# A gated pair of S4D convolutions on one core: phases rounded inside the matmul chain, decay grids on GpSimd, trig in place in PSUM

## The chip, the core and the metric

The kernel runs on one core of one Trainium2 chip. A core has a matrix engine (PE, with its weight loads, PEld), a vector engine (DVE), a scalar engine for functions (ACT), GpSimd (POOL) and a queue engine that only starts transfers (SP). Each runs its own instructions in order and waits for the others on semaphores. Matmuls write PSUM, of which there are eight banks of 512 float32 per partition; everything else lives in SBUF. The metric is the device time in microseconds of the whole program, from its first instruction to its last.

## The reference, cut to what matters

Two diagonal state space layers A and B see the same input x (2048 steps, 512 channels, 128 modes a channel) and are mixed by a gate for each step.

```python
def layer(u, log_A_real, A_imag, C_real, C_imag, log_dt, D_skip):
    dt = exp(log_dt)
    A = -exp(log_A_real) + 1j * A_imag
    C = (C_real + 1j * C_imag) * dt[:, None]
    P = exp((A * dt[:, None])[:, :, None] * arange(L))    # 512 x 128 x 2048
    K = 2 * einsum("dn,dnl->dl", C, P).real               # the filter
    y = irfft(rfft(u, 2 * L) * rfft(K, 2 * L))[:L]
    return y + u * D_skip
g = sigmoid((x * gate_w).sum(-1, keepdims=True))
return g * layer_A(x) + (1 - g) * layer_B(x)
```

## The kernel before, in words

A channel of one layer is a filter; there are 1024. They are worked off in 64 units of 16 filters (`u`), 16 blocks of four units (`b`), 8 chunks of eight units (`c`) and 4 super-blocks of four blocks (`sb`).

Each filter is split as step = 64 m + q. Modes lie on the partitions, so that the sum over modes is a matmul of two factors, f1 (32 values of m) and f0 (64 of q), each a decay times a cosine or sine.

- Per chunk, `prep_ops(c)` (line 153) turns the parameters into an amplitude, a decay rate and phase factors. The phase factors are split into three bfloat16 parts (`split`, `rest`), written to DRAM (`bounce`) and read back turned (`back`) into `rot`. Most of it is DVE work on 128x128 tiles, with some ACT. `make_bases` (284) makes 28 columns of exponentials on ACT in seven parts; `amplitudes` multiplies four of them on DVE.
- Per unit, `phase` (298) makes 1024 phases, in turns, with two matmuls of 512 columns (unit 0 takes another way, with nine). `turn` (315) converts them to int16 on ACT, `half` (319) casts that to fp16 on DVE, and `less` (322) subtracts the whole turns with two more matmuls. `sine`, `absf` and `cosine` (334 to 342) are ACT passes over 1024 elements into the SBUF tile `fsn`. `grid1` and `grid0` (345 to 359) multiply exponentials into decay grids of 512 and 1024 elements on DVE; `prod1`, `prod_minus`, `prod_cos` and `prod_sin` (362 to 385) multiply grids and trig on DVE, two SBUF operands each.
- `modes` (387) sums over the modes with 32-column matmul tiles; `keep` and `skip` evacuate; `s1_k` and `keep_x` do the first step of a transform.
- Per block, `s2` (443) does the second step, `products` (466) multiplies the spectrum of the filter by that of the input in `v`, once straight and once crossed, in one DVE instruction for each of eight groups; four accumulating DMAs from POOL's queue (`add_products`, 498) add the two halves; `inverse` and `keep_z` transform back. Every second block a new `v` is made: `keep_v`, two kinds of DMA and, on ACT, `negate_v`.
- Per super-block, `final` and `final_out` finish and write; the last super-block has its own end (`last_e` to `last_out`). The gate is a matmul (591), a sigmoid over 2048 elements and sixteen DMAs that spread it over the partitions.

PSUM before: two banks for the phases, one each for `pk`, `ps1` and `fin`, three shared by the rest. The order of PE, DVE and ACT is that of one list, sorted by a key for each operation (the table `AT`, offsets against the unit's or block's number); a dependency without a semaphore ties each instruction to the one before it on its engine. Transfers and POOL's few instructions keep the order in which that list reaches them.

Of the kernel before, what the change touches and what calls it, by code (L numbers as in the profile page):

```python
# [11 lines left out]
BF16 = mybir.dt.bfloat16  # L12
I32 = mybir.dt.int32
F16 = mybir.dt.float16
I16 = mybir.dt.int16
# [4 lines left out]

M = 32
# [7 lines left out]
BUFS = {"f1": 2, "f0": 2, "fsn": 2, "ph": 1, "pk": 1, "ps1": 1, "bg": 3, "fin": 1}  # L37

# [7 lines left out]
def tile_gated_s4d(ctx: ExitStack, tc: tile.TileContext, nsb, a, out):  # L46
    nc = tc.nc
    nblk = 4 * nsb
    nunit = 4 * nblk
    nchunk = 2 * nsb  # L50

    const = ctx.enter_context(tc.tile_pool(name="const", bufs=1))
    prep = ctx.enter_context(tc.tile_pool(name="prep", bufs=1))
    work = ctx.enter_context(tc.tile_pool(name="work", bufs=2))
    psum = ctx.enter_context(tc.tile_pool(name="psum", bufs=1, space=PSUM))
    dram = ctx.enter_context(tc.tile_pool(name="dram", bufs=2, space=DRAM))

    V, S, PE = nc.vector, nc.scalar, nc.tensor
    ops = []

    def op(name, home, fn, i=None, *args):
        at = AT[name] if i is None else AT[name][i]
        ops.append((home + at, len(ops), name, fn, args, (name, i), home))

    def op_at(name, key, fn, *args):
        ops.append((key, len(ops), name, fn, args, None, key))


    small = const.tile([128, nchunk + 1 + nsb], F32, name="small")
    nc.sync.dma_start(out=small, in_=a["small"])  # L70
    ldt, sgn, gw = small[:, 0:nchunk], small[:, nchunk : nchunk + 1], small[:, nchunk + 1 :]
    pars, uraws = {}, {}

    def load_pars(c):
        pars[c] = prep.tile([128, 4, 128], F32, name="par", tag="par")
        nc.sync.dma_start(out=pars[c], in_=a["par"][c])

    def load_u(b):
        uraws[b] = work.tile([128, 8, Q], F32, name="uraw", tag="uraw", bufs=1)
        nc.sync.dma_start(out=uraws[b], in_=a["us"][b])  # L80

    load_pars(0)
    warm = const.tile([128, 1], F32, name="warm")
    V.memset(warm, 0.0)
    S.activation(warm, warm, AF.Exp)
    ident = const.tile([128, 128], F32, name="ident")
    ph0 = work.tile([16, 3, 512], BF16, name="ph0", tag="f1", bufs=BUFS["f1"])
    nid = const.tile([128, 128], F16, name="nid")
    w1 = const.tile([128, 2, 128], F32, name="w1")
    cph = const.tile([96, 2, 512], BF16, name="cph")  # L90
# [3 lines left out]
    consts = [(ident, a["ident"]), (ph0, a["ph0"]), (nid, a["nid"]), (w1, a["w1"]), (cph, a["cph"])]  # L94
    consts += [(dl, a["dl"]), (mi, a["mi"])]
    consts += [(gk[:, j : j + 8], a["gk"][:, j : j + 8]) for j in range(0, M, 8)]
    for i, (o, x) in enumerate(consts):
        op("ld", 0, lambda o=o, x=x: nc.sync.dma_start(out=o, in_=x), i)


    v = const.tile([128, M, 128], F32, name="v")
# [6 lines left out]
    gs = const.tile([128, 2048], F32, name="gs")  # L108
    eg = const.tile([128, Q, 2, M], F32, name="eg")


# [40 lines left out]

    def prep_ops(c):

        d = {}

        def tiles():
            if d:
# [664 lines left out]
```

## Time and profile before

| | us |
|---|---|
| median of 3 runs | 607.37 (606.05 to 607.65) |
| the profiled execution: its span | 606.9 |
| of it: DVE busy | 505.4 |
| ACT busy | 502.6 |
| PE busy | 491.7 |
| POOL busy | 61.0 |

The profile is of one execution. Its span runs from the first to the last instruction; no longer time of that execution is given, so the span is its own time. Busy time is the time in which at least one instruction of the engine runs. Ends of matmuls are modelled, and a busy PE includes the filling of its array. In a view of groups, a row names the line, engine, operation, the tile written and those read, the shape and the count, then the busy time of the group in microseconds and the mean of one instruction in nanoseconds, then the idle time of the engine before them with what ended it. In a view of the timeline, a row starts with the start and the length in microseconds of one or more instructions of a line that ran without a gap.

### The profile page before, as it was taken

Reading aid. Unit: us, or ns where it says so; the run is one execution under the profiler, and the core shown is the slowest. Engines: PE = TensorE matmul, PEld = TensorE weight load, DVE = VectorE, ACT = ScalarE, POOL = GpSimd, SP = SyncE. Lnnn points to the kernel's source line nnn. Section 1 sums busy time; section 2 is a strip of 40 time slices with the busy share of each in tenths; the row PEclk is TensorE's granted clock in tenths of the full one; section 3 lists DMA queues with packets and bytes.
Section 4 is the critical chain, followed back from the end, with each engine's and each line's share of the span. In section 5 each row is a group of like instructions: output and inputs, shape, how many; then the busy total and the mean of one; then the engine's idle time right before and its main releaser. Section 6 shows DMA issues by size and latency. Waiting matters only on the chain.

```text
span 606.9 us, 22768 instructions
## 1 busy us (share of the span) xinstructions
PE 491.7 (81%) x10071; PEld 393.6 (65%) x10071; DVE 505.4 (83%) x872; ACT 502.6 (83%) x942; POOL 61.0 (10%) x72
## 2 busy tenths in 40 slices
PE   5587869695987969987695979998688888988756
PEld 4454747584775857776474857777466775767656
DVE  6599999977998978998799778998699786898930
ACT  3999998888998978799788989799698897786611
POOL 0000100202002100012002020020102020020720
PEclk9799999988898979999899888999699898999989
DMA  8956440635008260185306251073502651054441
GB/s 281 292 171 84 97 98 3 106 53 115 20 2 125 51 134 21 27 138 88 78 3 106 53 123 38 30 115 64 114 1 43 101 98 44 21 89 80 72 69 72
DMA packets 91923, 50.39 MB, mean 83 GB/s; under 512 B 75840, under 2 KB 80448, under 8 KB 91824
## 3 DMA queue, kind: packets, MB, share of 16 engines
q1 hardware_dynamic: 86704, 32.15, 23.1%
q0 software_dynamic: 5120, 16.78, 16.5%
q8 instruction: 79, 1.29, 0.9%
q14 instruction: 20, 0.16, 0.1%
HBM read 16.93 MB, written 5.77 MB: 37 GB/s over the span
## 4 chain that ended last, share of the span: by engine, by line
PE 18%; ACT 14%; DMA 13%; DVE 9%; issue 3%; POOL 1%; ACTq 0%; POOLq 0%; DVEq 0%
DMA xall<-xall 6%; DMA dsp<-sp 4%; PE psi L513 4%; PE ps L455 4%; DVE xall L468 3%; DMA rot<-dsp 3%; ACT bas L289 2%; PE pf L540 2%; ACT r L317 2%; PE pk L393 2%; DVE f L375 2%; PE ps L411 2%; ACT fsn L338 2%; PE ph L325 1%; ACT fsn L342 1%
## 5 line engine op out<-in xcount | busy, mean ns | idle before, releaser
L347 DVE TENSOR_TENSOR f<-bas 128x1024 f32<-128x1024 f32 (+1 forms) x128 | 119.0, 947 | 3.1 <-ACT bas L289 3.1
L455 PE MATMUL ps<-xall,gk 128*64 128x64 f32 (+1 forms) x1728 | 113.9, 252 | 5.5 <-ACT v L479 2.3
L455 PEld LDWEIGHTS ps<-xall,gk 128*64 128x64 f32 (+1 forms) x1728 | 102.9, 153 | 19.5 <-ACT v L479 4.0
L513 PE MATMUL psi<-mi,xall 128*128 128x128 f32 x512 | 80.9, 310 | 31.1 <-DMA xall<-xall 31.1
L502 POOL DMA_DIRECT2D xall<-xall x64 | 53.4, 1248 | 522.9 <-ACT r L317 188.9
L513 PEld LDWEIGHTS psi<-mi,xall 128*128 128x128 f32 x512 | 75.0, 221 | 41.4 <-issue 35.5
L468 DVE TENSOR_TENSOR xall<-ps,v 128x512 f32<-128x512 f32 x128 | 85.6, 683 | 6.1 <-PE ps L455 3.4
L317 ACT ACTIVATE r<-ph 128x1024 int16<-128x1024 f32 x64 | 67.0, 1047 | 25.3 <-PE ph L312 23.7
L411 PE MATMUL ps<-w,ks 128*64 128x128 f32 x1024 | 70.5, 280 | 15.3 <-DVE ks L405 8.1
L375 DVE TENSOR_TENSOR f<-f,fsn 128x1024 f32<-128x1024 f32 x64 | 78.0, 1220 | 1.4 <-ACT fsn L342 1.4
L363 DVE TENSOR_TENSOR f<-f,fsn 128x1024 f32<-128x1024 f32 x64 | 77.9, 1218 | 0.0
L393 PE MATMUL pk<-f,f 128*32 128x64 f32 x4096 | 75.3, 229 | 2.1 <-DVE f L385 1.0
L393 PEld LDWEIGHTS pk<-f,f 128*32 128x32 f32 x4096 | 64.4, 115 | 17.8 <-issue 6.1
L338 ACT ACTIVATE fsn<-ph 128x1024 f32<-128x1024 f32 x64 | 67.2, 1050 | 5.7 <-PE ph L325 5.6
L411 PEld LDWEIGHTS ps<-w,ks 128*64 128x64 f32 x1024 | 55.3, 138 | 25.0 <-DVE ks L405 10.2
L342 ACT ACTIVATE fsn<-fsn 128x1024 f32<-128x1024 f32 x64 | 69.8, 1091 | 0.3
L335 ACT ACTIVATE fsn<-ph 128x1024 f32<-128x1024 f32 x64 | 67.5, 1055 | 0.1
L289 ACT ACTIVATE bas<-dec 128x128 f32<-128x128 f32 x224 | 60.6, 482 | 0.1
L519 ACT COPY z<-psi 128x512 f32<-128x512 f32 x64 | 38.4, 617 | 25.5 <-PE psi L513 25.5
L320 DVE CAST r<-r 128x1024 f16<-128x1024 int16 x64 | 27.1, 423 | 37.0 <-ACT r L317 36.9
L312 PE MATMUL ph<-cph,rot 96*128 96x512 bf16 x126 | 39.2, 393 | 21.5 <-DMA rot<-dsp 15.5
L325 PE MATMUL ph<-r,nid 128*128 128x512 f16 x128 | 41.8, 410 | 15.9 <-DVE r L320 15.4
(102 smaller groups left out, 595.7 us busy)
## 6 DMA issues: line engine op xcount, KB each, us to landing
xall<-xall POOLq DMA_DIRECT2D x64, 256.0 KB, 6.5
v<-v SPq DMA_DIRECT2D x64, 128.0 KB, 4.5
uraw<-in_us SPq DMA_DIRECT2D x16, 256.0 KB, 3.5
z<-in_ut SPq DMA_DIRECT2D x16, 256.0 KB, 5.7
out_dram<-ot SPq DMA_DIRECT2D x24, 128.0 KB, 2.6
par<-in_par SPq DMA_DIRECT2D x8, 256.0 KB, 2.6
gk<-in_gk SPq DMA_DIRECT2D x4, 512.0 KB, 5.3
eg<-in_eg SPq DMA_DIRECT2D x4, 512.0 KB, 7.2
```

Of the source, the lines that this page charges most:

```text
L289: S.activation(bases[c][:, :, j], decays[c][:, 0], AF.Exp, scale=-float(s) if s else 0.0)
L317: S.activation(rs[u].bitcast(I16), phs[u], AF.Copy)
L338: S.activation(fsn(u)[:, 0], phs[u], AF.Abs)
L342: S.activation(f, f, AF.Sin, bias=HALF_PI, scale=-TWO_PI)
L347: V.tensor_tensor(o.rearrange("p k (a b) -> p k a b", b=8), bas[:, :, hi : hi + n].unsqueeze(3).to_broadcast([128, 16, n, 8]), bas[:, :, l ...
L363: V.tensor_tensor(f1s[u].rearrange("p v k m -> p v (k m)"), f1s[u][:, 1].rearrange("p k m -> p (k m)").unsqueeze(1).to_broadcast([128, 2, ...
L375: V.tensor_tensor(f0[:, :, :, 0:32], f0[:, 1, :, 0:32].unsqueeze(1).to_broadcast([128, 2, 16, 32]), back, OP.mult)
L393: PE.matmul(pk[32 * kd : 32 * kd + 32, i, :], f1[:, p, 4 * i + kd, :], f0[:, p, 4 * i + kd, :], start=p == 1, stop=p == 0, tile_position=( ...
L411: PE.matmul(ps[64 * ri : 64 * ri + 64, i, :], kss[u][:, i, :], w1[:, ri, :], start=True, stop=True, tile_position=(0, 64 * ri),)
L455: PE.matmul(ps[h : h + w, j, 0:n], gk[:, k, h : h + w], xall[:, x0:x1, 2 * k : 2 * k + 2], start=True, stop=True, tile_position=(0, h),)
L468: V.tensor_tensor(k.rearrange("p x (k t) -> p k x t", t=2), p2s[b, g][:, :, 0:64].unsqueeze(2).to_broadcast([128, 4, 2, 64]), v[:, 4 * g : ...
L513: PE.matmul(ps[:, i, :], xk(b)[:, x : x + 2, :].rearrange("p x k -> p (x k)"), mi, start=True, stop=True)
```

## The change

It rewrites most of the kernel around the same mathematics. What it does, part by part:

- Phases. They are rounded inside the accumulation: the matmul chain of each 512-element half adds 1.5 x 2^23, adds the phase, subtracts 1.5 x 2^23 and subtracts the phase again. `turn`, `half` and `less` go. Phase factors are two fp16 parts. The half that belongs to f0 uses rows 0 to 63 of the array, that of f1 rows 64 to 127; four matmuls each, alternating.
- Trig. Each half has one bank for its phases, in which the sine replaces them, and one for the absolute value, which the cosine replaces. The two banks change roles from unit to unit (`t0`, `t1` and `u0`, `u1`). The products read them there.
- Grids. `grid0` and `grid1` run on POOL, two SBUF operands each, and so do `amplitudes`; of the 28 exponentials the four with shift 0 are constants.
- Prep. Chunks 1 and 2, 3 and 4, 5 and 6 are prepared together; except for the first batch the arithmetic that touches no PSUM runs on POOL.
- `products` becomes two instructions for each group, straight and crossed; `v` is laid out in four planes; `negate_v` moves to DVE.
- The gate's matmul writes all 128 rows, the sigmoid works in PSUM, and its sixteen spreading DMAs go.
- PSUM: four banks for trig, one for `pk`, and three that all else takes in a listed turn (`SLOTS`). One list of 2494 numbers (`ORDER`) gives the order of all operations, and the ties without semaphore now also bind POOL's instructions and SP's transfers.

```diff
+ONE_W, ONE_M, LOW = 4096.0, 3072.0, 2048.0
+BATCHES = ((0,), (1, 2), (3, 4), (5, 6), (7,))
+ORDER = [
+    11, 6, 1, 3, 0, 2, 5, 4, 74, 45, 40, 50, 43, 41, 44, 46, 42, 18, 19, 20, 21, 22, 24, 12, 23,
...
+    def prep_ops(i):
+        cs = BATCHES[i]
+        w = len(cs)
+        E = V if i == 0 else G
...
+        def high():
+            S.activation(halves(0), both("tb"), AF.Copy)
+
+        def rest():
+            E.tensor_tensor(both("tb"), both("tb"), halves(0), OP.subtract)
...
+    def turns(c):
+        i = next(i for i, cs in enumerate(BATCHES) if c in cs)
+        for h, t in zip((0, 64), dsps[i]):
+            src = t[BATCHES[i].index(c)].rearrange("(u k) d n -> (k d) u n", u=8)
+            dma(rot[h : h + 32 * (1 + h // 64), c % 2], src)
+
+    def make_bases(c):
+        for j, s in enumerate(SHIFTS):
+            if s:
+                S.activation(bas[:, c % 2, :, j], decays[c][:, 0], AF.Exp, scale=-float(s))
...
     def phase(u):
-        for h in range(2):
-            PE.matmul(ph[:, 512 * h : 512 * h + 512], rot[:, u % 8, :], cph[:, h, :], start=True, stop=True)
+        p0s[u], p1s[u] = (bank(f"{k}{u % 2}", f"{k}{u % 2}") for k in "tu")
+        for j in range(4):
+            for h, ps in ((0, p0s[u]), (64, p1s[u])):
+                w = rot[:, u // 8 % 2, u % 8] if j % 2 else ones
+                PE.matmul(
+                    ps, w[h : h + 64], cph[h : h + 64, j], start=j == 0, stop=j == 3, tile_position=(h, 0)
+                )
+
+    def magnitude(u, ps, pc, k):
+        pc[u] = bank(f"{k}{1 - u % 2}", f"{k}{1 - u % 2}")
+        S.activation(pc[u], ps[u], AF.Abs)
+
+    def sine(u, ps):
+        S.activation(ps[u], ps[u], AF.Sin, scale=TWO_PI)
+
+    def cosine(u, pc):
+        S.activation(pc[u], pc[u], AF.Sin, bias=HALF_PI, scale=-TWO_PI)
...
     def grid(u, o, hi, n, lo):
-        V.tensor_tensor(
+        G.tensor_tensor(
...
+    def sin_plus(u):
         o = f0s[u][:, 1, :, 32:64]
-        V.scalar_tensor_tensor(o, o, -1.0, g0(u)[:, 1], op0=OP.mult, op1=OP.mult)
+        V.scalar_tensor_tensor(o, o, -1.0, half(u, p0s[u], False), op0=OP.mult, op1=OP.mult)
+
+    def one_cos(u):
+        f = f1s[u].rearrange("p v k m -> p v (k m)")
+        V.tensor_tensor(f[:, 0], f[:, 1], p1c[u], OP.mult)
...
+    def products(b, g, second):
+        x0 = 64 * (b % 2)
+        if second:
+            x0 = 32
+        k = xall[:, x0 : x0 + 32, 8 * g : 8 * g + 8]
+        vv = v[:, 2 * (b % 2) + second, 4 * g : 4 * g + 4, :]
...
+    def negate_v(i, h):
+        V.tensor_scalar(v_at(hi, i, 1, h), v_at(hi, i, 0, h), -1.0, None, op0=OP.mult)
...
+    def gate_sig(j):
+        S.activation(psg[j], psg[j], AF.Sigmoid, scale=sgn)
...
+    for n in ORDER or range(len(ops)):
+        key, name, fn, args = ops[n]
...
         for i in new:
-            if i.engine in (mybir.EngineType.PE, mybir.EngineType.DVE, mybir.EngineType.Activation):
-                if i.engine in last:
...
+            if i.engine in last:
...
+    cph = np.zeros((2, 64, 4, 512))
...
+    cph[:, 0, 0], cph[:, 0, 2] = ONE_M, -ONE_M
+    cph[:, :, 3] = -cph[:, :, 1]
```

More of the change, by code (lines that the diff above doesn't have):

```diff
@@ L93, in tile_gated_s4d @@
     mi = const.tile([128, 128], F32, name="mi")
[L94 to L101, printed above, removed]
+    v = const.tile([128, 4, M, 32], F32, name="v")
     xall = const.tile([128, 128, 2 * M], F32, name="xall")
@@ L144, in make_dt @@
         ]
[L147 to L174 removed]
+    als, decays, dsps = {}, {}, {}
@@ new lines, in prep_ops @@
+        return start + middle + [
+            add("t2", "t2", "rc"), high, rest, low, bounce,
+            mul("mx", "mx", "ax"), mul("ay", "ay", "sy"), diag, turned, dec,
+        ]
+    def turns(c):
[7 more added lines that the diff above has]
+                S.activation(bas[:, c % 2, :, j], decays[c][:, 0], AF.Exp, scale=-float(s))
```

719 lines of the change are left out of this document (345 added, 374 removed), and 153 rows, old and new, of the table ORDER.

## The prediction

> **What bounds it now.** I read the page's engine shares first, then the windows cut where the first and the last unit's mode products start (line 393, from its source view), then the groups kept apart by shape.
>
> ```profile
> span 606.9 us, 22768 instructions
> PE 491.7 (81%) x10071; PEld 393.6 (65%) x10071; DVE 505.4 (83%) x872; ACT 502.6 (83%) x942; POOL 61.0 (10%) x72
> L393 PE MATMUL pk<-f,f x4096: 218/219/316, 36.6 to 573.0; 128*32 128x64 f32 x196
> 0.00:36.60 36.60, 21.29 (x185) 14.49 (x188) 23.05 (x83) 26.13 (x61) 0.20 (x4) 0.91 0.88 280
> 36.60:572.10 535.50, 448.55 (x9387) 358.24 (x9386) 472.27 (x774) 466.78 (x864) 55.06 (x63) 0.95 0.38 71
> 572.10:607.00 34.90, 21.89 (x506) 20.88 (x504) 10.10 (x18) 9.71 (x19) 5.73 (x6) 0.90 0.26 62
> 151.70:221.90 70.20, 58.54 (x1127) 46.85 (x1126) 63.40 (x106) 65.27 (x118) 6.66 (x8) 0.94 0.37 66
> ```
>
> The columns of a window are its length, then the busy microseconds of PE, weight loads, DVE, ACT and POOL with instruction counts, granted clock, DMA share and GB/s. The reader is to see three stretches. The first 36.6 us load and prepare; the last 34.9 us are a chain of one block that has nothing beside it (PE 21.9, DVE 10.1, ACT 9.7). Between them lie 535.5 us for the 63 further units, 8.50 us each, where DVE (472.3) and ACT (466.8) are both 87 to 88% busy, PE 84% and POOL 10%. In the fullest chunk shown ACT reaches 65.27 of 70.20 us, 93%. So no engine waits for one culprit; two engines are nearly full, and the rest is what in-order queues lose to each other. The waits that one can name are small:
>
> ```profile
> PE psi L513 <- DMA xall<-xall: 31.1, 15, 7.4
> PE ph L312 <- DMA rot<-dsp: 15.5, 6, 3.9
> ```
>
> The first is mostly the last block's (7.4 of it) and the accumulating DMA's landing, which stays. The second is the phase factors returning from DRAM at the start of a chunk, six times; the new order prepares two chunks in one batch, so it should mostly go.
>
> **The change, engine by engine.** DVE first.
>
> ```profile
> L468 DVE TENSOR_TENSOR xall<-ps,v 128x512 f32<-128x512 f32 x128 | 85.6, 683 | 6.1 <-PE ps L455 3.4 <-DMA v<-v 2.4
> L375 DVE TENSOR_TENSOR f<-f,fsn 128x1024 f32<-128x1024 f32 x64 | 78.0, 1220 | 1.4 <-ACT fsn L342 1.4
> L363 DVE TENSOR_TENSOR f<-f,fsn 128x1024 f32<-128x1024 f32 x64 | 77.9, 1218 | 0.0
> L347 DVE TENSOR_TENSOR f<-bas 128x1024 f32<-128x1024 f32 x64 | 77.4, 1211 | 0.0
> L381 DVE TENSOR_TENSOR f<-f,fsn 128x512 f32<-128x512 f32 x64 | 43.9, 685 | 11.3 <-ACT fsn L342 11.1
> L385 DVE SCALAR_TENSOR_TENSOR f<-f,fsn 128x512 f32<-128x512 f32 x64 | 43.7, 682 | 0.0
> L347 DVE TENSOR_TENSOR f<-bas 128x512 f32<-128x512 f32 x64 | 43.6, 683 | 3.1 <-ACT bas L289 3.1
> L320 DVE CAST r<-r 128x1024 f16<-128x1024 int16 x64 | 27.1, 423 | 37.0 <-ACT r L317 36.9
> L244 DVE RECIPROCAL rc<-rc 128x128 f32<-128x128 f32 x8 | 7.5, 943 | 0.0
> L213 DVE TENSOR_TENSOR tb<-tb,sp 128x256 f32<-128x256 f32 x16 | 6.7, 420 | 0.0
> ```
>
> The two grids leave: 77.4 + 43.6 = 121.0. The cast of line 320 leaves: 27.1. The four trig products (77.9 + 78.0 + 43.9 + 43.7 = 243.5) become six of 512 elements, one operand in PSUM; line 468 has that form, 85.6/128 = 0.669 each, so 384 x 0.669 = 256.9: +13. Line 468's 128 products become 256 of 256 elements. No such form with PSUM is shown; bounds are half of line 468 (0.33, no change) and line 213's 0.42 for 256 elements, which I take: 107.5, +22. The prep on DVE, by windows over the whole run for lines 183, 187 and 190:
>
> ```profile
> 0.00:607.00 607.00, 24.08 (x88) 0.94 0.41 83
> 0.00:607.00 607.00, 8.83 (x40) 0.94 0.41 83
> 0.00:607.00 607.00, 9.02 (x32) 0.94 0.41 83
> ```
>
> That is 24.1 + 9.0 + 8.8, with lines 244 and 213 another 7.5 + 6.7: 56. Seven of eight chunks leave for POOL, 49, but per later batch three operations (0.42 each), a reciprocal of twice 943 ns, a sign pass (0.42) and a PSUM copy (0.67) stay: 4 x 4.3 = 17, so -32. The 32 negations of v come over from ACT, some 0.4 each: +14. DVE: -121 - 27 + 13 + 22 - 32 + 14 = -131, in the middle 472 becomes 341.
>
> ACT:
>
> ```profile
> L342 ACT ACTIVATE fsn<-fsn 128x1024 f32<-128x1024 f32 x64 | 69.8, 1091 | 0.3
> L335 ACT ACTIVATE fsn<-ph 128x1024 f32<-128x1024 f32 x64 | 67.5, 1055 | 0.1
> L338 ACT ACTIVATE fsn<-ph 128x1024 f32<-128x1024 f32 x64 | 67.2, 1050 | 5.7 <-PE ph L325 5.6
> L317 ACT ACTIVATE r<-ph 128x1024 int16<-128x1024 f32 x64 | 67.0, 1047 | 25.3 <-PE ph L312 23.7 <-PE ph L306 1.2
> L289 ACT ACTIVATE bas<-dec 128x128 f32<-128x128 f32 x224 | 60.6, 482 | 0.1
> L418 ACT COPY xall<-ps 128x512 f32<-128x512 f32 x64 | 38.8, 606 | 1.3 <-PE ps L411 1.3
> L490 ACT ACTIVATE v<-v 64x512 f32<-64x512 f32 x32 | 18.3, 619 | 0.3
> ```
>
> Line 317's conversion leaves; sine, absolute value and cosine of 1024 become six passes of 512 from PSUM to PSUM. Before: 69.8 + 67.5 + 67.2 + 67.0 = 271.5. After: 384 at line 418's 0.606 (a 512 read from PSUM) = 232.7, so -39. The bounds are half of line 335 (0.527, 202: -69) and 0.67 where each cosine waits for its own absolute value with nothing between (257: -14). Of 28 exponentials a chunk four fall away: 60.6 x 32/224 = -8.7. Negations: -18.3. ACT: -66, the middle 467 becomes 401.
>
> PE:
>
> ```profile
> 162.58 0.59 PE L312 MATMUL ph<-cph,rot 96*128 96x512 bf16 x2 [0.21 <-ACT fsn L335]
> 163.99 1.10 PE L393 MATMUL pk<-f,f 128*32 128x64 f32 x64
> 165.08 0.59 PE L325 MATMUL ph<-r,nid 128*128 128x512 f16 x2
> 553.16 1.40 PE L455 MATMUL ps<-xall,gk 128*64 128x64 f32 x32
> ```
>
> A unit now has two pairs of 512 columns (phase and its correction), 0.59 + 0.59 = 1.18 us. It gets eight of 512 columns, alternating between the upper and lower 64 rows. In a pair the second adds 0.59 less one matmul's 0.38 to 0.39 = 0.21. If the halves run side by side there are four steps, 0.59 + 2 x 0.21 = 1.01: -11 us over 64 units. If not, 0.59 + 6 x 0.21 = 1.85: +43. No row shows row groups; the nearest shows column groups: 64 products of 64 columns in four column groups take 1.10 (17 ns each), 32 in two groups 1.40 (44 ns each), so groups of the array do overlap. I take -11: PE 449 becomes 438.
>
> POOL:
>
> ```profile
> L502 POOL DMA_DIRECT2D xall<-xall x64 | 53.4, 1248 | 522.9 <-ACT r L317 188.9 <-ACT ot L549 127.8 <-ACT v L479 78.4
> L561 POOL MEMSET el<- 128x2048 f32 x4 | 8.0, 2135 | 1.8 <-DVE f L375 1.2 <-PE pk L393 0.6
> ```
>
> POOL has done no arithmetic. Per unit it gets 1536 grid elements. Low bound: DVE's own 121 us. High bound: two reads and a write one after another, each at the memset's 2135/2048 = 1.04 ns an element: 3.13 x 1536 x 64 = 307. I take the middle, 214, since the operation is DVE's row and the engine the memset's. The prep's 24,200 elements cost 41 (line 213's rate) to 76: 58; the amplitudes 9. With the 55 of now: 336, bounds 226 to 447. Idle POOL time (480 of 535) covers this; without that cover it would appear in every unit. Two queues change with it. The DMA issues of line 502 now stand behind grids on POOL: late by one grid, some 2 us, in a block of 34 us. DVE's products now wait for POOL's grids, and behind a late one stand the block's own products and so PE. On SP the phase factors take 26 transfers for 16 and the gate 16 fewer; a chunk ahead, as the listed order has them after the first, none of these is on the path.
>
> The Trainium skill, GPSIMD Engine Reference, Performance versus the Vector engine, gives 4497 ns for a two-input operation of 2048 elements, about twice DVE, because two inputs share one read port; worked out as an estimate from that page the grids take 216 us.
>
> A rule speaks against putting arithmetic on POOL, and rows bear on it:
>
> ```profile
> 565.35 4.07 POOL L561 MEMSET el<- 128x2048 f32 x2
> 567.56 1.22 DVE L363 TENSOR_TENSOR f<-f,fsn 128x1024 f32<-128x1024 f32 x1
> 570.54 2.45 DVE L566 COPY el<-eg 64x512 f32<-64x512 f32 x2
> 570.63 2.08 POOL L561 MEMSET el<- 128x2048 f32 x1 [1.22 <-DVE f L375]
> ```
>
> DVE's single-source copies (2.45 us for two) lasted as long as POOL's memset, while the two-input product at 567.56 took its usual 1.22 beside another. So some DVE forms and POOL do exclude each other. In the new middle such forms are the 32 negations and a few sign passes; a wait of up to one 1024 grid (some 2 us) for 32 of them is at most 64 us of DVE's 194 us of slack, and a delay of the v chain that a block's length hides.
>
> The Trainium skill, SBUF — State Buffer, SBUF: two separate sides, calls this an exclusive lock on a shared port pair, and adds DVE operations with two SBUF inputs against a POOL operation that reads SBUF. By that page today's products would be blocked, the new ones, which read one operand from PSUM, not; no row here has POOL reading SBUF.
>
> **Sum.**
>
> ```profile
> 24.73 3.00 ACT L289 ACTIVATE bas<-dec 128x128 f32<-128x128 f32 x12
> ```
>
> Start and end keep 36.6 + 34.9 = 71.5: the tail's chain is the same, with 16 products for eight (at most +2). In the start the first unit's phases now wait for the DRAM round trip, but its exponentials hold ACT until 27.7 us anyway; I allow 5 us either way. In the middle the two fullest engines averaged (472.3 + 466.8)/2 = 469.5 for 535.5 us. Now the fullest two are PE 438 and ACT 401, mean 420. The same proportion gives 535.5 x 420/469.5 = 479; half of the 15.5 us of returning factors comes off, since the rest is already in the proportion: 471. Span 71.5 + 471 = 542.5, and with the 0.5 by which the median of the runs shown (607.37) stands above this span, 543 us.
>
> **The rivals.**
>
> (a) PE's busy time holds the fill of each group; weight loads are 358 of its 449 in the middle. If a busier PE packs groups, ACT sets the end: 401/0.92 (near its fullest chunk) = 436, in all 508.
>
> (b) The row halves do not run side by side: PE 449 + 43 = 492, at 93% full 529: 600; by the proportion with ACT's 401, 509 - 8: 573. About 587. For it: eight wide products where four were. Against: the column groups above.
>
> (c) Slower: the in-place banks. A unit's cosine lives in the bank that the next unit's phase is written to, so phase, three ACT passes on one half, two on the other, and two DVE products make a loop: 1.01 + 5 x 0.61 + 2 x 0.67 = 5.4 us. The loop of now is phase 0.59, conversion 1.05, cast 0.42, correction 0.59 and two ACT passes 2.1: 4.75, and runs at 8.50, so 3.75 are queueing. If that queueing stays, the pace is 9.15 and the time 71.5 + 63 x 9.15 = 648. It decides from 3.1 us of waits a unit. For it: with one bank set, nothing of the next phase can be done ahead, and PE's in-order queue makes other blocks' products wait behind it. Against: the 3.75 came from two engines 88% full, which now are 64 and 75%.
>
> (d) POOL costs over three times DVE's grid time (over 5.7 us a unit): its queue is the bound; at four times, 484 + 122 = 606 in the middle, 670 or more in all.
>
> (e) POOL and DVE exclude each other in all forms: 341 + 336 = 677, in all 749. The 1.22 at 567.56 speaks against it.
>
> **Chances.** Forecast 0.55, (a) 0.17, (b) 0.10, (c) 0.10, (d) 0.05, (e) 0.03. Under 0.3%, about 1.8 us, a run cannot be told from no change. Faster: forecast, (a) and 0.08 of (b), 0.80; the same 0.03; slower 0.17. The range goes from 503, (a) with the start 5 us shorter, to 603, which takes in (b) and leaves out (c) to (e). The likeliest case alone spans 520 to 563: ACT between its bounds (371 and 426, so 525 to 558 by the proportion) and the start's 5 us.
>
> **What would show it.** DVE near 374 us in all, ACT near 437, PE 470 to 495, POOL 330 to 400; a phase group of eight in 1.0 us (wrong at 1.8); a unit pace of 7.5 us between mode products; negations of 2 us beside grids of 1.9 to 4.8 us a pair. Waits of ACT on PE's phase, or of PE's phase on DVE's products, of over 3 us a unit would show (c). Start or end longer by over 5 us would break the sum outside the middle.

## The result and the profile after

The changed kernel takes 573.65 us, median of 4 runs (572.76 to 576.81), against 606.85 us of the kernel before on the same chip (606.05 to 607.65, 4 runs): ratio 0.946, 95% interval 0.9433 to 0.9486. That is 33 us faster, where 64 were forecast: the direction is right, and half of the gain is missing.

Page and windows of the changed kernel's profiled execution, cut where the first and the last unit's mode products (now line 572) start. The columns of a window are those of the prediction.

```profile
span 571.5 us, 23861 instructions
PE 490.1 (86%) x10352; PEld 395.2 (69%) x10352; DVE 396.6 (69%) x826; ACT 430.8 (75%) x964; POOL 343.9 (60%) x324
0.00:38.60 38.60, 27.49 (x310) 23.94 (x310) 22.08 (x66) 25.16 (x62) 17.07 (x23) 0.96 0.49 151
38.60:534.40 495.80, 435.63 (x9495) 345.64 (x9493) 364.73 (x738) 395.15 (x883) 321.72 (x297) 0.96 0.37 83
534.40:571.50 37.10, 26.98 (x554) 25.58 (x552) 9.76 (x23) 10.50 (x19) 5.11 (x5) 0.90 0.31 68
```

Start and end are 2.0 and 2.2 us longer than before. The middle took 495.8 us, 7.87 a unit; 471 and 7.5 were forecast. Its busy times, on the other hand, are near the forecast: PE 435.6 (438), ACT 395.2 (401), DVE 364.7 (341). So the terms of these three were priced well, and what they were turned into was not. The groups, kept apart by shape, say the same:

```profile
L521 POOL TENSOR_TENSOR f<-bas 128x1024 f32<-128x1024 f32 x64 | 126.7, 1981 | 119.4 <-PE pk L572 100.9 <-DVE f L560 5.6 <-issue 3.8
L521 POOL TENSOR_TENSOR f<-bas 128x512 f32<-128x512 f32 x64 | 72.1, 1133 | 22.3 <-issue 11.8 <-DVE xall L638 4.5 <-PE pk L572 4.4
L544 DVE TENSOR_TENSOR f<-f,t 128x512 f32<-128x512 f32 x64 | 43.7, 683 | 12.6 <-ACT t L517 12.3
L638 DVE TENSOR_TENSOR xall<-ps,v 128x256 f32<-128x256 f32 x256 | 96.3, 417 | 34.2 <-PE ps L627 32.4 <-ACT u L511 0.7
L658 DVE TENSOR_SCALAR v<-v 64x512 f32<-64x512 f32 x32 | 19.6, 635 | 1.7 <-ACT v L647 1.1
L511 ACT ACTIVATE u<-u 128x512 f32<-128x512 f32 x64 | 37.8, 591 | 33.4 <-PE u L505 29.6 <-DVE f L564 3.8
L757 PE MATMUL psg<-z,small 128*128 128x512 f32 x32 | 16.5, 664 | 0.2 <-ACT xall L601 0.2
```

And the timeline of PE for one unit's phases (start, length, then the operation):

```profile
400.74 0.37 PE L505 MATMUL t<-cph,ones 64*128 64x512 f16 x1 [0.45 <-DVE f L548]
400.75 0.39 PE L505 MATMUL u<-cph,ones 64*128 64x512 f16 x1
400.96 0.37 PE L505 MATMUL t<-cph,rot 64*128 64x512 f16 x1
400.97 0.38 PE L505 MATMUL u<-cph,rot 64*128 64x512 f16 x1
...
401.40 0.38 PE L505 MATMUL u<-cph,rot 64*128 64x512 f16 x1
```

The two row halves start 0.01 us apart and the steps are 0.21 to 0.22 us: a group of eight takes 1.04 us (400.74 to 401.40 + 0.38).

**Where the middle went: a ledger of PE.** PE was busy 448.6 of 535.5 us before and 435.6 of 495.8 after. What it waited for, summed by releaser over the rows of its waits view in the middle (they account for 84.9 of 86.9 and for 58.8 of 60.2 us of idle time):

| us in the middle | before | forecast | after |
|---|---|---|---|
| length | 535.5 | 471 | 495.8 |
| PE busy | 448.6 | 438 | 435.6 |
| PE not busy | 86.9 | 33 | 60.2 |
| of it: waits for DMA | 39.1 | | 1.5 |
| waits for DVE | 26.6 | | 31.3 |
| waits for ACT | 19.2 | | 14.0 |
| waits for nothing the profile shows ("issue") | 0 | | 12.0 |

The main rows behind it, first of the kernel before, then of the changed one (total us, times, longest):

```profile
PE psi L513 <- DMA xall<-xall: 23.6, 14, 3.5
PE ph L325 <- DVE r L320: 15.4, 22, 1.6
```

```profile
PE t L505 <- DVE f L544: 8.3, 6, 1.8
PE pf L696 <- issue: 7.0, 4, 2.9
PE pk L572 <- issue: 2.9, 3, 1.9
PE psi L676 <- DMA xall<-xall: 0.6, 1, 0.6
```

The ledger says where the time went, not yet why. The 39.7 us that the middle lost are 13.0 of PE's own work and 37.6 of its waits for transfers, less 12.0 of a new kind of gap (the run no_accum, below, shows what PE waits for in it). DVE lost 108 us of work in the middle and ACT 72, yet what PE waits for the two of them together stayed: 45.8 before, 45.3 after. Within that, the waits for the cast (15.4) went with the cast, and others on DVE came in their place, first among them those for the phase banks (8.3). The missing 25 us are all PE idle time (60.2 for 33).

By place, the middle is not even. Windows of the changed kernel:

```profile
226.00:256.00 30.00, 28.80 (x624) 23.54 (x625) 24.78 (x50) 24.29 (x52) 16.29 (x14) 1.00 0.37 71
291.00:339.00 48.00, 45.14 (x917) 36.67 (x915) 41.89 (x80) 39.91 (x86) 28.01 (x25) 1.00 0.28 56
339.00:367.00 28.00, 21.82 (x520) 19.32 (x516) 10.40 (x25) 24.10 (x74) 16.12 (x21) 0.82 0.34 75
256.00:291.00 35.00, 29.01 (x862) 24.03 (x852) 20.45 (x43) 18.90 (x39) 15.99 (x13) 0.95 0.49 106
505.00:520.00 15.00, 11.48 (x376) 9.45 (x366) 7.04 (x15) 6.94 (x16) 6.22 (x5) 0.77 0.53 119
38.60:72.00 33.40, 27.23 (x507) 17.50 (x506) 22.04 (x40) 23.69 (x47) 31.50 (x30) 0.90 0.77 248
```

In the first two PE is 94 to 96% busy at full clock, and units follow each other in some 6 us on average. In the third PE has 21.82 of 28.00, ACT 24.10, and the clock is down to 0.82. In the fourth and fifth no engine is over 83%, DMA is at 0.49 and 0.53, and the clock at 0.95 and 0.77. In the sixth POOL has 31.50 of 33.40: the first batch's prep and the grids of units 1 to 4. The third window, seen on ACT's timeline:

```profile
339.80 1.28 ACT L489 ACT_TABLE_LOAD   x1
341.09 6.40 ACT L489 ACTIVATE bas<-dec 128x128 f32<-128x128 f32 x24
...
350.18 5.85 ACT L489 ACTIVATE bas<-dec 128x128 f32<-128x128 f32 x24
...
360.20 1.28 ACT L517 ACT_TABLE_LOAD   x1
361.49 0.58 ACT L517 ACTIVATE u<-u 128x512 f32<-128x512 f32 x1
```

Both chunks of a batch get their 24 exponentials here, with the function tables changed before and after (1.28 us each). For 21.7 us no sine or cosine of a unit is made, and the phases of two units lie 25.8 us apart. The same pair stands at 78.88 to 96.76.

### The profile page after: what moved, and what is told of

Read it like the earlier page. It is cut to its first block, busy times and chain, and to the rows that moved or that the text cites. A ratio compares the mean times of both kernels' runs of the same rounds, so it can differ in the third digit from the quotient of the medians.

```text
span 571.5 us, 23861 instructions
## 1 busy us (share of the span) xinstructions
PE 490.1 (86%) x10352; PEld 395.2 (69%) x10352; DVE 396.6 (69%) x826; ACT 430.8 (75%) x964; POOL 343.9 (60%) x324
## 4 chain that ended last, share of the span: by engine, by line
PE 50%; ACT 21%; DVE 15%; issue 6%; POOL 5%; DMA 3%; DVEq 0%; SPq 0%; ACTq 0%; POOLq 0%
PE ps L627 11%; PE ps L591 9%; PE psi L676 9%; PE t L505 7%; ACT bas L489 6%; PE pk L572 6%; PE pf L696 4%; DVE xall L638 3%; ACT u L511 2%; POOL f L521 2%; ACT u L517 2%; ACT t L511 2%; DVE f L548 2%; PE pw L287 1%; PE pl L730 1%
## 5 line engine op out<-in xcount | busy, mean ns | idle before, releaser
L521 POOL TENSOR_TENSOR f<-bas 128x1024 f32<-128x1024 f32 (+1 forms) x128 | 195.0, 1557 | 141.7 <-PE pk L572 105.3
L638 DVE TENSOR_TENSOR xall<-ps,v 128x256 f32<-128x256 f32 x256 | 96.3, 417 | 34.2 <-PE ps L627 32.4
L560 DVE TENSOR_TENSOR f<-f,u 128x512 f32<-128x512 f32 x64 | 43.7, 683 | 56.8 <-ACT u L517 46.9
L591 PE MATMUL ps<-w,ks 128*64 128x128 f32 x1024 | 69.8, 280 | 12.7 <-DVE ks L582 5.0
L511 ACT ACTIVATE u<-u 128x512 f32<-128x512 f32 x64 | 37.8, 591 | 33.4 <-PE u L505 29.6
L505 PE MATMUL t<-cph,ones 64*128 64x512 f16 x128 | 50.4, 394 | 12.3 <-DVE f L544 8.3
L544 DVE TENSOR_TENSOR f<-f,t 128x512 f32<-128x512 f32 x64 | 43.7, 683 | 12.6 <-ACT t L517 12.3
L505 PE MATMUL u<-cph,ones 64*128 64x512 f16 x128 | 50.4, 393 | 1.5 <-DVE f L560 1.5
L505 PE MATMUL t<-cph,rot 64*128 64x512 f16 x128 | 49.9, 390 | 0.0
L505 PE MATMUL u<-cph,rot 64*128 64x512 f16 x128 | 49.7, 388 | 0.0
L511 ACT ACTIVATE t<-t 128x512 f32<-128x512 f32 x64 | 38.2, 596 | 13.5 <-DVE f L552 6.4
L548 DVE TENSOR_TENSOR f<-f,t 128x512 f32<-128x512 f32 x64 | 43.6, 681 | 6.1 <-ACT t L517 5.7
```

The costliest lines, as they stand in the source:

```text
L505: PE.matmul(ps, w[h : h + 64], cph[h : h + 64, j], start=j == 0, stop=j == 3, tile_position=(h, 0))
L511: S.activation(pc[u], ps[u], AF.Abs)
L521: G.tensor_tensor(o.rearrange("p k (a b) -> p k a b", b=8), x[:, :, hi : hi + n].unsqueeze(3).to_broadcast([128, 16, n, 8]), x[:, :, lo : ...
L544: V.tensor_tensor(f0[:, 0, :, 0:32], f0[:, 1, :, 0:32], half(u, p0c[u], True), OP.mult)
L548: V.tensor_tensor(f0[:, 0, :, 32:64], f0[:, 1, :, 32:64], half(u, p0c[u], False), OP.mult)
L591: PE.matmul(ps[64 * ri : 64 * ri + 64, i, :], x[:, n0 + i, :], w1[:, ri, :], start=True, stop=True, tile_position=(0, 64 * ri),)
```

## The experiments

Each edit is made to the changed kernel. The last column is the ratio less 0.946, times 606.85: what the edit does to the changed kernel. The halves of the intervals are 0.004 to 0.009, so effects under some 5 us are not told from nothing, and those of 6 us stand at the edge of that. "The forecast's rule" in the expectations is the prediction's proportion with the changed kernel's own factor: 1.19, its middle of 495.8 us over the mean of 435.6 and 395.2, where the prediction had 535.5/469.5 = 1.14.

| run | median us | ratio to before, interval | edit's effect, us |
|---|---|---|---|
| spread | 584.61 | 0.9641, 0.9561 to 0.972 | +11 |
| prep_dve | 579.63 | 0.9562, 0.952 to 0.9605 | +6 |
| pe_less | 576.71 | 0.9505, 0.9457 to 0.9554 | +3 |
| rows_serial | 575.67 | 0.949, 0.9439 to 0.954 | +2 |
| no_bursts | 567.74 | 0.9369, 0.9285 to 0.9454 | -6 |
| act_less | 576.85 | 0.9509, 0.9439 to 0.958 | +3 |
| grids_dve | 624.61 | 1.0293, 1.0209 to 1.0378 | +51 |
| pool_more | 593.02 | 0.9783, 0.9708 to 0.9858 | +20 |
| pe_more | 585.88 | 0.9679, 0.9605 to 0.9754 | +13 |
| dve_less | 571.97 | 0.944, 0.9372 to 0.9507 | -1 |
| less_three | 567.26 | 0.9368, 0.9289 to 0.9448 | -6 |
| no_accum | 557.8 | 0.9207, 0.9149 to 0.9266 | -15 |

To see where an effect arises, here is the time by which a unit's product of line 564 (`one_sin`, one of its six) starts earlier or later than in the changed kernel, by the profiled execution of each run; us. That execution was the fastest of the four in no_bursts, pool_more and no_accum and the slowest in prep_dve.

| unit | changed kernel starts at | spread | prep_dve | no_bursts | pool_more | grids_dve | no_accum |
|---|---|---|---|---|---|---|---|
| 4 | 63.3 | +0.1 | +3.5 | -0.1 | +5.0 | 0.0 | -0.1 |
| 6 | 98.2 | -4.6 | +4.3 | -4.7 | +7.8 | 0.0 | -1.0 |
| 10 | 128.4 | +6.5 | +5.0 | -2.6 | +9.4 | +3.1 | -1.0 |
| 24 | 232.0 | +5.0 | +5.8 | -5.8 | +10.3 | +20.9 | -1.7 |
| 38 | 333.3 | +5.6 | +7.8 | -5.9 | +12.9 | +30.1 | -9.6 |
| 40 | 366.6 | +1.4 | +9.6 | -12.3 | +12.7 | +30.3 | -9.8 |
| 46 | 403.9 | +9.8 | +9.0 | -10.1 | +16.5 | +36.0 | -10.1 |
| 60 | 503.2 | +9.1 | +7.9 | -10.7 | +18.3 | +52.5 | -12.0 |
| 62 | 528.3 | +9.0 | +8.8 | -10.9 | +18.6 | +54.2 | -17.1 |

**spread: the two exponential bursts of a batch pulled apart**

```diff
+def _place(op, after):
+    ORDER.remove(op)
+    ORDER.insert(ORDER.index(after) + 1, op)
+
+for _pair in ((452, 462), (453, 481), (1638, 1685), (1639, 1703)):
+    _place(*_pair)
```

452 and 1638 are the exponentials of chunks 2 and 6, 453 and 1639 their amplitudes; they now follow units 8 and 42.

> Theory A (bursts): the middle is 25 us longer than forecast because ACT makes the 24 exponentials of both chunks of a batch within 21 us of each other (339.8 to 361.5), with no trig pass between, so phases of two units lie 25.8 and 22.6 us apart there where 6 to 7 is usual. Here the second chunk's exponentials of batches 1 and 3 are made two to three units later. By A some 15 us of the two long gaps come back, less two more pairs of table loads (4 x 1.28 = 5.1 us of ACT): 560 to 567 us. Theory B (POOL, 94% busy from 38.6 to 72 us and 92% to 98, is late with grids and prep): no change, 571 to 577. Theory C (PE alone sets the pace at 88% busy, and its other matmuls fill the gaps anyway): 570 to 576.

It was slower, 584.61 us. The gaps shrank where the bursts had been paired (-4.6 at unit 6, 4.2 gained from 38 to 40), but each moved burst cost more in its new place: 11.1 us from unit 6 to 10, 8.4 from 40 to 46. A burst on its own is 6.2 us with 2.6 of table loads around it, and units wait for all of that. All three theories had it at 577 or below. A had the place right, since both gaps shrank, and the remedy wrong.

**prep_dve: prep of the first two later batches back on DVE**

```diff
-        E = V if i == 0 else G
+        E = V if i < 3 else G
```

> The arithmetic of the prep of batches 1 and 2 (chunks 1 to 4) goes back from POOL to DVE, same places in the order. Theory B (POOL late in the first 150 us): some 30 us leave POOL there, and 6 to 10 us of the time: 563 to 568. Theory A (exponential bursts): at most 3 us, 570 to 575. Theory C (PE sets the pace): no change, 572 to 576.

Slower by 6, of which 3.5 are there by unit 4. In the stretch where POOL is fullest, taking its prep away does not help: from 38.6 to 72 us DVE is then busy for 29.38 us instead of 22.04, and PE waits 7.9 us for it instead of 5.5. Theory B, as a remedy, is out.

**pe_less: half of the phase matmuls**

```diff
-        for j in range(4):
+        for j in (1, 3):
...
-                    ps, w[h : h + 64], cph[h : h + 64, j], start=j == 0, stop=j == 3, tile_position=(h, 0)
+                    ps, w[h : h + 64], cph[h : h + 64, j], start=j == 1, stop=j == 3, tile_position=(h, 0)
```

> Leaves out four of the eight phase matmuls of a unit (the two that add and subtract 1.5 x 2^23), so phases are not rounded and the output is not the reference's. PE loses two steps of 0.22 us and their share of the fill, some 0.45 us a unit, 29 us in all. Theory C (PE sets the pace): 541 to 552. Theory A (bursts) and the prediction's rule that the two fullest engines share the pace: half of it or less, 557 to 568. Theory B (POOL): under 5 us, 569 to 575.

No gain. PE's busy time fell by 14.7 us and not by 29, since the rest of its work grew. These rows are from the page and the groups of this run; line 591 is a transform's first step that the edit doesn't touch, 69.8 us and 280 ns in the changed kernel:

```profile
PE 475.4 (83%) x10096; PEld 392.1 (68%) x10096; DVE 394.7 (69%) x826; ACT 430.4 (75%) x964; POOL 343.7 (60%) x324
L591 PE MATMUL ps<-w,ks 128*64 128x128 f32 x1024 | 73.7, 288 | 19.5 <-issue 7.5 <-DVE ks L582 5.6 <-ACT z L682 2.7
38.60:539.00 500.40, 422.10 (x9248) 343.11 (x9249) 363.66 (x738) 394.90 (x883) 321.57 (x297) 0.93 0.37 82
```

The granted clock of the run is 0.929 where the changed kernel had 0.958. The lighter PE idles more, is granted less clock, and gives part of the saving back. Its waits in the middle rose from 58.8 to 76.2 (DVE 40.5 for 31.3, issue 18.7 for 12.0). So C falls: PE's busy time alone does not set the middle.

**rows_serial: the row halves issued one after the other**

```diff
-        for j in range(4):
-            for h, ps in ((0, p0s[u]), (64, p1s[u])):
+        for h, ps in ((0, p0s[u]), (64, p1s[u])):
+            for j in range(4):
```

> The four matmuls of the upper half are issued first, then the four of the lower half; before they alternate. If alternation is what lets the row halves run side by side, a group of eight takes 1.04 + 3 x 0.21 = 1.7 us or more instead of 1.04, so PE gains 40 us or more. Theory C (PE sets the pace): 605 to 620. The prediction's rule (the mean of the two fullest, times 1.19): 574 + 0.5 x 40 x 1.19 = 598, so 590 to 602. Theory A (bursts): up to 590. If the order within the group doesn't matter: 574.

No change: 575.67. PE's timeline of this run shows why:

```profile
401.27 0.37 PE L505 MATMUL t<-cph,ones 64*128 64x512 f16 x1 [0.45 <-DVE f L548]
401.29 0.39 PE L505 MATMUL u<-cph,ones 64*128 64x512 f16 x1
401.49 0.37 PE L505 MATMUL t<-cph,rot 64*128 64x512 f16 x1
401.52 0.38 PE L505 MATMUL u<-cph,rot 64*128 64x512 f16 x1
```

The first product of the lower half, fifth as the kernel is written, starts 0.02 us after the first of the upper half and before its second. The trace does not hold the order in which PE was given them. The weight loads do follow another order than in the changed kernel (ones, rot, ones, rot, where that has ones, ones, rot, rot), which speaks against the halves having been put back in turn before they reached PE. The run could not price rival (b), because the halves could not be made to queue this way; whether they can be made to was not tried.

After these four, theory D took the middle as a row of stretches with different limits.

**no_bursts: exponentials of six chunks left out**

```diff
-            if s:
+            if s and c < 2:
```

> Leaves out the 24 exponentials of chunks 2 to 7 (the grids then use those of chunks 0 and 1). ACT loses 6 x 6.2 = 37 us and two pairs of table loads, 5.1 us. Theory D (formed after the first four runs: the middle is a row of stretches with different limits; in stretches of some 103 us in all around the exponentials ACT is 94 to 99% busy and PE, which is 95% busy elsewhere, can't use the time, so a burst costs its whole length): 42 us less, 529 to 540. The forecast's rule (half of what one of the two fullest engines loses, times 1.19): 25 us less, 546 to 552. Theory C (PE sets the pace throughout): 565 to 574.

6 us by the medians, 11 in the two profiled executions (560.5 and 571.5), not 42. The table by unit shows 4.7 at unit 6 and 6.4 between 38 and 40, the two paired bursts, and some 4 in all at the three single ones (10 to 24, and 46 to 60). Of the first pair only one burst is left out, that of chunk 2. So the pairs do cost, some 9 to 11 us of profile time together, of which 2 are lost again after unit 6, and the rest of the bursts was hidden. D's price of "the whole length" is wrong. In the middle (38.6 to 523.5) PE's busy time fell as well, with no PE work removed:

```profile
38.60:523.50 484.90, 429.02 (x9488) 342.02 (x9476) 363.89 (x737) 354.60 (x735) 320.84 (x297) 0.98 0.38 85
```

429.0 us at clock 0.98, where it was 435.6 at 0.96; the product of the two is the same within 1%. A stall of PE is paid twice, as idle time and as slower matmuls after it. The clock right behind one shows it: PE stood still until 284.67 us, the next 4 us were granted 0.58, and the clock was 1.00 again after them (windows of the changed kernel):

```profile
284.60:288.60 4.00, 3.93 (x32) 3.64 (x33) 0.48 (x1) 0.96 (x3) 0.41 (x1) 0.58 0.85 182
288.60:292.00 3.40, 3.40 (x85) 2.57 (x89) 0.17 (x1) 2.56 (x5) 0.00 (x0) 1.00 0.02 5
```

**act_less: one of six trig passes left out**

```diff
-            ("c1", lambda u: cosine(u, p1c)), ("s1", lambda u: sine(u, p1s)),
+            ("c1", lambda u: None), ("s1", lambda u: sine(u, p1s)),
```

> Leaves out the cosine pass of the f1 half (64 passes of 0.59 us, 38 us of ACT; the products then take the absolute value), the same amount of ACT as the bursts, but spread evenly over the units. Theory D: it counts only where ACT is the limit, some 8 us around the bursts and up to 10 in the mixed stretches: 555 to 566. The forecast's rule: 22 us less, 549 to 554. ACT the limit of every unit: 536 to 540. Theory C: 570 to 575.

No gain from 30 us less of ACT's busy time (400.4 for 430.8). D and the forecast's rule both expected one. ACT's load, spread over the units, has no price here that can be told.

**grids_dve: both grids back on DVE**

```diff
-        G.tensor_tensor(
+        V.tensor_tensor(
```

> Both grids go back from POOL to DVE; the rest stays. DVE gains 121 us (64 x 1.89), 365 + 119 = 484 in the middle, POOL keeps some 145 us. Theory D (the fullest engine at 95%): the middle 484/0.95 = 510, in all 586. The forecast's rule: (484 + 436)/2 x 1.19 = 547, in all 623. If POOL's grids, late, are what holds the middle: under 574. It also shows whether the negations on DVE, 635 ns here, take some 0.4 us when POOL makes no grids.

624.61 us, slower than the kernel before. This one move carries the change: without it, in this order, the rest makes the kernel 3% slower. The forecast's rule hit (623) with its factor of 1.19; with the prediction's own 1.14 it gives 600. DVE is the fullest engine here: with it busy 465.4 of 549.4 us, PE's waits for DVE rise from 31.3 to 67.0. Its waits for transfers are gone here too, and the kernel is slow all the same. Negations, from the source view of their line, first in the changed kernel, then here (shortest, median, longest in ns):

```profile
L658 DVE TENSOR_SCALAR v<-v x32: 408/424/3027, 36.0 to 502.8; 64x512 f32<-64x512 f32 x32
```

```profile
L658 DVE TENSOR_SCALAR v<-v x32: 418/424/878, 36.4 to 555.2; 64x512 f32<-64x512 f32 x32
```

The median is the same, and only beside POOL's grids do single ones take up to 3.03 us.

**pool_more: each f1 grid made twice on POOL**

```diff
         grid(u, f1s[u][:, 1], 24, 4, 16)
+        grid(u, f1s[u][:, 1], 24, 4, 16)
```

> Each f1 grid is made twice on POOL, 64 x 1.13 = 72 us more of POOL. Theory D: it counts only where POOL is full, units 1 to 7 (38 to 98 us, 93% busy): 6 or 7 units x 1.13, 579 to 584. POOL the limit of the middle: 610 or more. POOL with slack everywhere: 572 to 576.

Slower by 20: 9 by unit 10, where POOL is full, as D had it, and another 9 spread over the rest, where POOL is 59% busy in the changed kernel and 71% here. POOL does not set the middle (72 us more of it cost 20), but it has not the free slack that its share suggests.

After eight runs, theory E: PE has least slack with the loop from phase over ACT and DVE back to the bank close behind it.

**pe_more: two more pairs of phase matmuls**

```diff
-        for j in range(4):
+        for n, j in enumerate((0, 1, 0, 1, 2, 3)):
...
-                    ps, w[h : h + 64], cph[h : h + 64, j], start=j == 0, stop=j == 3, tile_position=(h, 0)
+                    ps, w[h : h + 64], cph[h : h + 64, j], start=n in (0, 2), stop=n in (1, 5), tile_position=(h, 0)
```

> Each half's chain of phase matmuls is begun twice (the first two steps are made, then the bank is started again), so a unit has six pairs where it had four and the result is the same. PE gains two steps of 0.22 us a unit, 28 us. Theory E (formed after eight runs: in the full stretches PE is the engine with the least slack, with the loop from phase over ACT and DVE back to the bank close behind; what is taken off one of them is taken up by the next, and what is added to PE counts whole): 596 to 604. The forecast's rule (half, times 1.19): 590 to 592. PE with slack: 574 to 580.

585.88 us lies between the ranges of the theories, nearest to that of the forecast's rule: slower by 13, half of the 28. PE's busy time rose by 22.1 (512.2), and its waits in the middle fell from 58.8 to 50.4.

**dve_less: one of six trig products left out**

```diff
-            ("os", one_sin), ("mo", modes), ("ke", keep), ("kd", skip), ("f1", first_k), ("xk", keep_x),
+            ("os", lambda u: None), ("mo", modes), ("ke", keep), ("kd", skip), ("f1", first_k), ("xk", keep_x),
```

> Leaves out the sine product of the f1 half (64 of DVE's products, 43.7 us; the grid is used in its place). Theory E: under 8 us, 566 to 575. DVE the limit of the units: 530 to 540. The forecast's rule, by which DVE is third and doesn't count: 574.

571.97: no change that can be told, with 37.5 us less of DVE (359.1 for 396.6). DVE is not the limit of the units; on E and the forecast's rule this run can't decide.

**less_three: the three of them together** (the edits of pe_less, act_less and dve_less)

> Leaves out three things together: the rounding steps of the phase (28 us of PE at full clock), the cosine pass of the f1 half (38 us of ACT) and its sine product (44 us of DVE). Theory E: what each alone did not give (the first two gave 0) they give together, since no engine of the loop is left to take it up; PE's busy time in the middle falls by some 20 and its waits for DVE and ACT by 5 to 10: 543 to 555. Something outside the three (POOL, transfers, the hand-written order itself) sets the middle: 566 or more. The forecast's rule: (416 + 357)/2 x 1.19 = 460 for the middle, in all 536.

Only 6 us, 567.26, with 21, 32 and 39 us less busy time on PE, ACT and DVE. E falls, by its own bound. In the middle (38.6 to 527.9) PE is busy 21 us less and idle 15 us more:

```profile
38.60:527.90 489.30, 414.51 (x9244) 337.62 (x9242) 326.41 (x675) 363.14 (x820) 320.96 (x297) 0.94 0.38 84
```

What sets the middle is none of the three loads. What stays the same in this run is the hand-written order, the transfers, POOL and the chains between engines.

**no_accum: the accumulating transfers of 14 of 16 blocks left out**

```diff
-        G.dma_start(out=xk(b)[o, s], in_=t2[t, s], accum_op=OP.add)
+        if b in (0, 15):
+            G.dma_start(out=xk(b)[o, s], in_=t2[t, s], accum_op=OP.add)
```

> Leaves out the accumulating DMAs of blocks 1 to 14 (56 of 64; the two halves of the spectrum are then not added). PE shows 12 us in the middle in which it waits for nothing that the profile shows, 2.58 us at 282.09 and 2.89 us at 509.99 in the midst of a row of equal matmuls, both while the transfers are 90% busy. If these gaps come from the traffic of the accumulating DMAs, they go: 560 to 566. If they have another cause: 570 to 575, with the gaps still there. If the transfers also delay the chain of a block: under 558.

The largest gain of any run, 15 us. 557.8 lies at the upper edge of "under 558", by which the transfers also delay a block's chain; the gaps shrank and did not all go. The table by unit shows it in three places: 7.9 us from unit 24 to 38 and 5.1 from 60 to 62, about the fourth and fifth of the windows above, with some 2 more between 46 and 60. PE's gaps there, in the timeline of the changed kernel and of this run, at the same place of the program:

```profile
281.13 0.97 PE L696 MATMUL pf<-z,eg 64*32 64x64 f32 x50
284.67 0.65 PE L696 MATMUL pf<-z,eg 64*32 64x64 f32 x14 [2.58 <-issue]
285.25 3.31 PE L676 MATMUL psi<-mi,xall 128*128 128x128 f32 x16
```

```profile
276.77 0.98 PE L697 MATMUL pf<-z,eg 64*32 64x64 f32 x54
278.83 0.38 PE L697 MATMUL pf<-z,eg 64*32 64x64 f32 x10 [1.08 <-issue]
279.14 2.05 PE L677 MATMUL psi<-mi,xall 128*128 128x128 f32 x16
```

The gap stands in the midst of 64 equal products; with the transfers it is 2.58 us, without them 1.08, and the 16 inverse products behind it take 3.31 and 2.05. The gap at 509.99 has no counterpart here, though it is less plainly one beside these transfers: in it their queue took 1% of the DMA engines' time and the other queue 48%, where the expectation speaks of 90%. Over the middle, "issue" gaps fall from 12.0 to 3.2 and PE's busy time from 435.6 to 429.0, at a clock of 0.98 for 0.96:

```profile
38.60:517.30 478.70, 429.03 (x9490) 341.35 (x9478) 359.93 (x737) 394.24 (x883) 274.15 (x242) 0.98 0.21 56
```

The middle is 17.1 us shorter: 8.8 are "issue" gaps, 6.6 PE's busy time, and the waits for DVE fell by 2.5. The edit also takes the issues of these transfers, 47.5 us, off POOL; a freer POOL would show as shorter waits for DVE, so it explains little of the gain. Without the accumulating transfers, then, PE's stalls that no semaphore explains are shorter.

What PE waits for in them can be read from the trace's DMA packets. The page of the changed kernel lists a queue for instructions (packets, MB, share of the DMA engines):

```profile
q8 instruction: 81, 1.33, 0.9%
```

81 packets of 16 KB go with 20,704 matmuls and weight loads, one for 256 of them; pe_less, with 20,192, has 79, and pe_more, with 21,216, has 83. So this queue carries PE's instructions. In the changed kernel nine gaps of over 0.3 us are put down to "issue", and each ends 1.28 to 1.55 us after such a packet has landed: the one that ends at 284.67 after the packet from 282.35 to 283.23, the one that ends at 512.88 after that from 510.68 to 511.60. The four of this run end 1.20 to 1.58 us after one. Of the 50 gaps as long that end with a named engine or transfer, 2 lie so. In these gaps, then, PE waits for its own instructions. The order seems to have a part in it: in the 5 us before four of the nine gaps PE began 400 to 442 matmuls and weight loads, most of them in rows of 64-column products, where no 5 us of the kernel before hold more than some 355, and that kernel has no such gap in its middle. Neither spreading these rows nor moving the transfers was tried. The transfers can't be left out of a useful kernel, and no run that does all the work was faster than the changed kernel.

## Why the prediction was half right

**Right, by its own steps.** The busy times: ACT 430.8 in all (437 forecast, six passes of 0.59 us for 0.606), PE 490.1 (481), POOL 343.9 (336, within 226 to 447), DVE 396.6 (374). POOL's total is near by some luck: the grids took 198.8 for 214, the prep 83 for 58, over its bound of 76. The row halves do run side by side, so rival (b) is out: 1.04 us for a group, 1.01 forecast. The waits for returning phase factors are gone, 15.5 before and none in the waits view after. Rivals (c) to (e), all of them slower, did not come: PE waits for the banks of the t half 12.2 us in the middle (line 505 on 544, above, and on 548, 3.9), and ACT for the phases of the u half 29.6 (line 511), 0.2 and 0.5 us a unit where (c) needed 3.1. Rival (a), PE packing its groups, would have needed the idle time to vanish.

Of the skill's rules, the Trainium skill, GPSIMD Engine Reference, Performance versus the Vector engine, gave 216 us by estimate; the trace has 126.7 + 72.1 = 198.8, 8% less. The Trainium skill, SBUF — State Buffer, SBUF: two separate sides, has DVE wait in certain forms beside POOL: the 3.03 us negation beside grids, 0.88 at most without them, agrees, and the products that read PSUM keep their 0.68 us, which agrees too.

**Off in size, without effect.** DVE came out 23 us above the forecast, though its block products took less (96.3 for 107.5), trig products 262 for 257 and negations 19.6 for 14. The rest is the subtraction itself: groups that run back to back overlap, so the groups of before add up to 565 us for 505.4 of busy time, those of after to 429 for 396.6, and taking whole groups off a busy time takes off too much. PE came out 9 above: 6.2 in the start, where the warm-up doubled (14.6 for 7.2), and 5.1 in the end, where 72 inverse products fall instead of 42; in the middle it was 2.4 below, although the gate's matmul, now 128 rows wide, takes 16.5 us where it took 4.1 (664 ns each for 601, and four times as many columns of weights). The prediction counted the gate's DMAs only.

**The step that failed** is "The same proportion gives 535.5 x 420/469.5 = 479". It makes the middle shrink in proportion to the mean busy time of the two fullest engines. Two things in it were wrong.

- It changed engines on the way: before, the two were DVE and ACT; after, PE and ACT. PE, at 84%, was already nearly as full as they and was to lose only 11 us. With PE and ACT on both sides the same rule gives 535.5 x 419.5/457.7 - 8 = 483, half of the 25 us that are missing.
- It holds that idle time shrinks with work. The runs show that it doesn't: taking 15 to 38 us of busy time from PE, ACT or DVE alone changes the time by -1 to +3 us, from all three together by -6. The waits of PE for DVE and ACT stayed at 45 us. What fell was its own work, 13 us, and its waits for transfers, 37.6, for which the prediction had allowed 8 and of which it said that the larger part "stays". That row was misread: of its 31.1 us only 7.4 are the last block's, and 23.6 lie in the middle, where 0.6 are left. So most of the idle time that went stood in rows that the prediction had called small. That is a ledger and not a cause: grids_dve has no waits for transfers either, and its middle is 549.4 us.

What the runs show in its place: the waits for DVE and ACT stayed at 45.3 us, more than the 33 that the proportion left for all idle time, and 12.0 us came in which PE waits for its instructions (run no_accum), of which the kernel before had none. Together they are 57.3 of the 60.2 us of idle time. The proportion is not wrong everywhere: with DVE as the fullest engine, in grids_dve, it came within 2 us once it had the changed kernel's factor.

Two loads that come in bursts have a price of their own, 15 us for the accumulating transfers and about 6 for the exponentials of six chunks. These are no sum for the missing 25: the kernel before had such transfers and exponentials too, and the two were not left out together.

Open: why the waits for DVE and ACT did not shrink with their work, and why three engines, made lighter together, give 6 us; in that run PE's waits for DVE rose to 37.7 and its "issue" gaps to 15.1. A new order list, made for the lighter loads, would tell the order from the chains, and was not tried.

## What to carry to other kernels

Keep a ledger of the engine that will be fullest after the change, its work and its waits by releaser, and ask of each wait whether the change removes it; work taken from other engines is worth only the waits that it causes there. Do not scale idle time with busy time, least of all in a kernel whose order is written out by hand: here adding work cost 13 us for 28, while removing as much gave nothing. Work that comes in bursts, like all exponentials of two chunks or a bunch of transfers, is to be looked for by place, since an even average hides it. So are rows of many small matmuls, in which PE can run out of instructions.

## What was not expected of the hardware

- Matmuls on different row halves of the array start side by side even when all of one half are written before the other's: 401.27 and 401.29 in run rows_serial, for the first and the fifth in the program.
- PE's clock makes idle time cost more than itself. The windows with stalls above were granted 0.77 to 0.95 against 1.00 in full ones, and 4 us behind a stall of 2.58 us 0.58; with half of the phase matmuls gone the mean clock fell from 0.958 to 0.929, and 29 us less work became 15 us less busy time and no gain.
- PE stands still in the midst of a row of equal matmuls, up to 2.89 us, in stretches in which the DMA engines move much; 12.0 us in the middle, 3.2 without the accumulating transfers. Each of these gaps ends 1.2 to 1.6 us after a 16 KB packet of the instruction queue has landed.
